# Sixteen chunks of gated linear attention in one block of 64x64 quarters, with loads issued in front of output stores

## The chip, the cores and the metric

The kernel runs on one core of a Trainium2 chip. The metric is the device time of one execution in microseconds, lower being better. Before the change the median of three runs is 465.62 us (464.9 to 467.0). Each engine of the core has its own queue of instructions: TensorE (PE, and PEld for its weight loads), VectorE (DVE), ScalarE (ACT), GpSimd (POOL) and SyncE (SP), which here only starts transfers.

## The reference

Two blocks stand one behind the other. The first is a gated linear attention with a state of 48x48 for each of 8 heads in 4 sequences of 768 positions; the second is a feed-forward block that multiplies two projections.

```
# attention, for each sequence and head
for t in range(S):
    state = alpha[t][:, None] * state + einsum(k[t], v[t])   # outer product
    y[t]  = einsum(q[t], state)
# x: (4*768, 8*48) = (3072, 384)
a = x @ w1;  b = x @ w2          # 384 -> 1024
out = (a * b @ w3) @ w_out       # 1024 -> 1024 -> 384
```

The weights of the second block come as float64 words; the kernel makes fp32 values from them and splits each into three parts, so that its large products run as exact sums of fp32r products.

## The kernel before, in words

**Chunks.** The 4 x 768 positions are cut into 24 chunks of 128 (C = 128, six chunks a sequence). The 8 heads of a chunk are 4 pairs (NP = 4): head 2j + i of pair j lies in half i of the 128 partitions, 48 of 64 used. In a chunk, cumulative sums of log alpha give a decay for every position; k divided and q multiplied by these decays make the recurrence into plain products:

- `transposed(n)`: k and q of the chunk are transposed on TensorE (L381) and copied to SBUF by ScalarE (L383, tile qkT);
- scores: k by q for each head, masked to the causal triangle by VectorE (tile ms);
- values: y = v by the masked scores, plus state by q, both summed in PSUM;
- `outer(n)`: k by v (L393), added to the state T by VectorE (L401, L403); `advance` scales the state by decays on GpSimd at every second chunk;
- ScalarE copies y out of PSUM (tile x, L489), and SyncE stores it to DRAM (tile xd, transposed as the second block wants it).

**The loop.** Lines 689 to 786 run steps n = 0 to 24. In step n the scores of chunk n are made, and the values of chunk n − 1, whose state and masked scores come from the step before. Then come the transposes of chunk n + 1, the state's update, the decays of chunk n + 3 and pieces of the second block (`run`, generators in `fill`, matmuls at L515), which fill TensorE while a chunk's small operations wait for other engines. The number of pieces goes by `n`, so some steps are long (27 matmuls of 128x384, L515) and some have none. After step 24 a second part runs only the second block.

**Chunks 8 to 23.** From TURNED = 8 on, scores use 64 x 64 pieces of TensorE, so that the quarter of the causal square that is all zero is never computed. A chunk's square is cut at position 64 into early keys and late keys: early keys meet all 128 queries, late keys only the late 64. A matmul on 64 rows and 64 columns takes one quarter of the array; the rows are the half of the partitions that its operands lie in, the columns the half of the partitions that its output goes to. Before the change step n has these groups on TensorE, in this order:

- `attend_state(n - 1)`, L474: 8 matmuls, state by q, 64 wide out, 128 columns moving, one after the other in all four quarters;
- `turned_scores(n)`, L430: for each pair, early keys (128 columns moving) and late keys (64 columns). Head i writes bank `sc[i]`, the late keys in the other half of the partitions;
- `attend_low(n - 1)`, L419, in between: early values of the early queries, 64 rows, 64 columns moving;
- `transposed(n + 1)`, L381;
- `attend(n - 1)`, L482: values of the late queries from both halves at once, 128 rows, 64 columns moving;
- `outer(n)`, L393.

For the odd heads the two halves of ms are swapped, so GpSimd makes a swapped copy of their v (`turn_v`, L167, tile vt, two buffers). Masks are four VectorE operations a chunk (L440), since the halves have different triangles. In all of this, operands in the upper half of the partitions write one PSUM bank (`y[0]`, `sc[0]`), and those in the lower half another (`y[1]`, `sc[1]`).

**Order and waits.** The source order is the order in which work is handed to a scheduler, which places instructions on each engine and sets semaphores; each engine then runs its own queue in order. PSUM has eight banks, shared by all matmuls in turn: a matmul into a bank waits until the bank's earlier content was read. `later` holds stores to be issued; `store()` empties it on SyncE. It stands at the head of the step for n = 0, 1 and from FIRST = 6 on, before the loads of alpha, k, q and v for the following chunks (`load_a`, `load_kq`, `load_v`).

Of the kernel before, what the change touches and what calls it, by code (L numbers as in the profile page):

```python
# [10 lines left out]
FP32 = mybir.dt.float32  # L11
# [37 lines left out]
def kernel(  # L49
# [30 lines left out]
    PAIRED = 8  # L80
    TURNED = 8
    assert D <= DP and DM % C == 0 and DF % CW == 0 and S % C == 0 and N % G == 0
    assert DM <= 512 and TG <= 512
# [80 lines left out]
    def turn_v(n):  # L164
        if turned(n):
            for half in range(2):
                nc.gpsimd.tensor_copy(out=vts[n % 2][ds(DP * half, DP), :, 0:D],  # L167
                                      in_=st["v", n][ds(DP * (1 - half), DP), 1::2, 0:D])

# [37 lines left out]
    keep_bc = keep[:, None, :].to_broadcast([C, NP, C])  # L207
    for half in range(2):
        nc.gpsimd.tensor_copy(out=keep_turned[ds(DP * half, DP), 1 - half], in_=keep[ds(DP * half, DP), ds(DP * half, DP)])
    nc.gpsimd.memset(keep_turned[DP:, 1], -1)  # L210
    for x in qks:
# [202 lines left out]

    def attend_low(n, jj, i, half):

        s, w = ds(DP * i, DP), (vts[n % 2] if i else st["v", n])
        h = half * NP // 2 + jj
        nc.tensor.matmul(st["y", n][0][i][ds(DP * half, DP), jj, 0:DP], w[s, h if i else 2 * h, :],  # L419
                         st["ms", n][s, i, h, 0:DP], start=(n % NCH == 0 and jj == 0), stop=True, skip_group_check=True)  # L420

    def turned_scores(n):

        qkT = st["qkT", n]
        sc = [bank().rearrange("p (j c) -> p j c", j=NP) for _ in range(2)]
        for j in range(NP):
            for part in range(2):
                for i in range(2):
                    r, t = ds(DP * i, D), slice(DP * part, C)
                    nc.tensor.matmul(sc[i][ds(DP * (part ^ i), DP), j, t], qkT[r, 0, j, ds(DP * part, DP)],  # L430
                                     qkT[r, 1, j, t], start=True, stop=True)
            if turned(n - 1):
                for i in range(2):
                    attend_low(n - 1, j % 2, i, i ^ (j < 2))
        ms = work.tile([C, 2, NP, C], FP32, tag="ms", name="ms")
        for i in range(2):
            r = ds(DP * i, DP)
            low, high = (keep_turned[r, 0], keep_turned[:, 1]) if i else (keep[r, 0:DP], keep[:, DP:])
            for x, mask, t in ((slice(DP * i, DP * (i + 1)), low, slice(0, DP)), (slice(0, C), high, slice(DP, C))):
                masked = nc.vector.tensor_tensor(ms[x, i, :, t].bitcast(I32), sc[i][x, :, t].bitcast(I32),  # L440
                                                 mask[:, None, :].to_broadcast([x.stop - x.start, NP, DP]),
                                                 op=ALU.bitwise_and)
        ends_of_part1[0] = mark["ms", n] = masked.ins
        st["ms", n] = ms

    def scores(n):
        if turned(n):
            return turned_scores(n)
        qkT = st["qkT", n]
        sc = [bank().rearrange("p (j c) -> p j c", j=NP) for _ in range(2)]  # L450
        for j in range(NP):
            for i in range(2):
                r = ds(DP * i, D)
                nc.tensor.matmul(sc[i][:, j, :], qkT[r, 0, j, :], qkT[r, 1, j, :], start=True, stop=True)  # L454
        ms = work.tile([C, 2, NP, C], FP32, tag="ms", name="ms")
        for i in range(2):
            masked = nc.vector.tensor_tensor(ms[:, i].bitcast(I32), sc[i].bitcast(I32), keep_bc, op=ALU.bitwise_and)  # L457
        ends_of_part1[0] = mark["ms", n] = masked.ins
        st["ms", n] = ms
# [17 lines left out]
    def attend(n):  # L477
        (y, heads), ms, vc = st.pop(("y", n)), st.pop(("ms", n)), st.pop(("v", n))
        for j, i, to in heads:
            if turned(n):  # L480
                w = vts[n % 2][:, j, :] if i else vc[:, 2 * j, :]
                nc.tensor.matmul(to[:, DP:], w, ms[:, i, j, DP:], start=False,  # L482
                                 stop=(j % HP == HP - 1), skip_group_check=True)
            else:
                nc.tensor.matmul(to, vc[:, 2 * j + i, :], ms[:, i, j, :], start=(n % NCH == 0 and j % HP == 0),  # L485
                                 stop=(j % HP == HP - 1), skip_group_check=True)
        x = work.tile([C, HP, 2, C], FP32, tag="x", name="x", bufs=4)
# [201 lines left out]
    for n in range(N + 1):  # L689
        if not 1 < n < FIRST:  # L690
            store()
# [13 lines left out]
        if n >= FIRST:  # L705
            load_v(n + 2)
        if n:
            attend_state(n - 1)
        if n < N:
            scores(n)  # L710
        else:
            for j in range(NP):
                for i in range(2):
                    attend_low(n - 1, j % 2, i, i ^ (j < 2))
        transposed(n + 1)
# [32 lines left out]
        turn_v(n)  # L748
        if n:
            attend(n - 1)  # L750
# [126 lines left out]
```

## Time and profile before

| what | value |
|---|---|
| median of three runs | 465.62 us |
| the profiled execution | 464.49 us |
| its span in the trace | 462.8 us |
| TensorE busy | 446.9 us, 97% |
| VectorE busy | 371.7 us, 80% |
| ScalarE busy | 276.4 us, 60% |
| GpSimd busy | 95.1 us, 21% |
| x copies L489, 128x256 | 48, 384 ns each |
| swapped copies of v L167, 64x192 | 32, 557 ns each |
| stores of x | 48 of 96 KB, 3.9 us to landing |

How to read it: the profile is one execution. A group's line names the source line, the engine, the operation, output and inputs by the program's tile names, the shape and the count, then busy time, mean duration in ns and idle time in front of it with what ended it. In a timeline a row has its start, its length, and the number of records that were merged; an fp32 matmul has two records. In a table by windows each engine has its busy time and in brackets its instructions, and then come TensorE's clock as a share of full speed, the share of the transfer engines, and GB/s. A line of waits has engine, line and who was waited for, then total us, times, and the longest. Since engines run side by side, a busy time is no share of the span by itself: what counts is which engine the others wait for.

### The profile page before, as it was taken

Reading aid. Unit: us, or ns where it says so; the run is one execution under the profiler, and the core shown is the slowest. Engines: PE = TensorE matmul, PEld = TensorE weight load, DVE = VectorE, ACT = ScalarE, POOL = GpSimd, SP = SyncE. Lnnn points to the kernel's source line nnn. Section 1 sums busy time; section 2 is a strip of 40 time slices with the busy share of each in tenths; the row PEclk is TensorE's granted clock in tenths of the full one; section 3 lists DMA queues with packets and bytes.
Section 4 is the critical chain, followed back from the end, with each engine's and each line's share of the span. In section 5 each row is a group of like instructions: output and inputs, shape, how many; then the busy total and the mean of one; then the engine's idle time right before and its main releaser. Section 6 shows DMA issues by size and latency. Waiting matters only on the chain.

```text
span 462.8 us, 11150 instructions
## 1 busy us (share of the span) xinstructions
PE 446.9 (97%) x4296; PEld 423.2 (91%) x4296; DVE 371.7 (80%) x610; ACT 276.4 (60%) x544; POOL 95.1 (21%) x186
## 2 busy tenths in 40 slices
PE   4998999999999999999999999999999999999996
PEld 2675699898999989999999999999999999999996
DVE  2779997999979988999998999997542967776671
ACT  4685975767658563988875676764545443333430
POOL 6234232325414430121221201212010000000000
PEclk9999999999999999999999999999999999999999
DMA  9999999999999974466856446412115875665511
GB/s 173 254 208 228 261 224 192 248 209 219 184 227 193 234 165 138 130 224 212 235 178 196 146 128 177 149 52 86 51 48 153 243 210 180 186 178 159 166 51 52
DMA packets 148869, 80.37 MB, mean 174 GB/s; under 512 B 97392, under 2 KB 138608, under 8 KB 148816
## 3 DMA queue, kind: packets, MB, share of 16 engines
q1 hardware_dynamic: 143040, 64.44, 57.3%
q0 software_dynamic: 5776, 15.22, 11.0%
q8 instruction: 34, 0.56, 0.5%
q14 instruction: 19, 0.16, 0.1%
HBM read 57.58 MB, written 22.06 MB: 172 GB/s over the span
## 4 chain that ended last, share of the span: by engine, by line
PE 88%; DVE 4%; DMA 4%; ACT 2%; issue 1%; SPq 0%; DVEq 0%; ACTq 0%
PE bank L515 72%; DMA kq<-in_q_dram 3%; PE bank L381 3%; PE bank L430 3%; PE bank L482 2%; PE bank L474 2%; PE bank L340 1%; PE bank L393 1%; PE bank L346 1%; PE bank L454 1%; PE bank L343 1%; PE bank L419 1%; DVE qk L359 1%; DVE ms L457 1%; PE bank L485 1%
## 5 line engine op out<-in xcount | busy, mean ns | idle before, releaser
L515 PE MATMUL bank<-x,w 128*128 128x384 f32 x1152 | 210.2, 337 | 1.7 <-ACT qkT L383 1.1
L515 PEld LDWEIGHTS bank<-x,w 128*128 128x128 f32 x1152 | 200.2, 188 | 4.1 <-ACT qkT L383 1.4
L515 PE MATMUL bank<-w3o,ab 128*128 128x384 f32 x576 | 100.2, 336 | 0.0
L515 PEld LDWEIGHTS bank<-w3o,ab 128*128 128x128 f32 x576 | 99.9, 188 | 0.0
L540 ACT ACTIVATE bank<-bank 128x384 f32<-128x384 f32 x96 | 45.6, 476 | 43.4 <-PE bank L515 43.1
L524 ACT ACTIVATE t<-bank 128x384 f32<-128x384 f32 x64 | 31.9, 499 | 54.9 <-PE bank L515 54.9
L590 POOL DMA_DIRECT2D abd<-ab x45 | 25.8, 573 | 137.9 <-DVE ab L576 121.3
L383 ACT COPY qkT<-bank 128x512 f32<-128x512 f32 x48 | 26.2, 596 | 24.8 <-PE bank L381 24.8
L641 DVE TENSOR_TENSOR ab<-abl,ab 128x1024 fp32r<-128x1024 f32 x24 | 29.3, 1223 | 12.3 <-ACT ab L640 12.3
L640 ACT ACTIVATE ab<-abl 128x1024 fp32r<-128x1024 f32 x24 | 25.5, 1061 | 20.2 <-PE bank L515 18.4
L515 PE MATMUL bank<-wo,w3T 128*128 128x384 f32 x192 | 35.9, 334 | 0.0
L576 DVE TENSOR_TENSOR ab<-bank,r 128x384 f32<-128x384 f32 x44 | 24.1, 548 | 12.5 <-PE bank L515 6.3
L515 PEld LDWEIGHTS bank<-wo,w3T 128*128 128x128 f32 x192 | 33.5, 188 | 0.0
L249 ACT ACTIVATE power<-power,rebias 128x512 uint32<-128x512 uint32 (+1 forms) x36 | 25.3, 701 | 12.6 <-DVE power L248 12.4
L359 DVE TENSOR_TENSOR qk<-kq,e 128x768 f32<-128x768 f32 x24 | 23.1, 964 | 11.3 <-ACT e L350 7.9
L526 DVE SCALAR_TENSOR_TENSOR o<-bank,t 128x384 f32<-128x384 f32 x24 | 13.4, 557 | 23.0 <-issue 13.7
L642 DVE SCALAR_TENSOR_TENSOR ab<-ab,abl 128x1024 fp32r<-128x1024 f32 x24 | 29.2, 1217 | 0.0
L526 DVE SCALAR_TENSOR_TENSOR r<-bank,t 128x384 f32<-128x384 f32 x40 | 22.0, 550 | 6.8 <-PE bank L515 3.4
L251 DVE SCALAR_TENSOR_TENSOR mant<-mant,rest 128x512 f32<-128x512 uint32 (+1 forms) x36 | 23.4, 649 | 3.7 <-ACT rest L244 3.7
L252 DVE SCALAR_TENSOR_TENSOR power<-raw,power 128x512 uint32<-128x512 uint32 (+1 forms) x36 | 23.5, 653 | 2.4 <-ACT power L249 2.4
L253 DVE TENSOR_TENSOR mant<-mant,power 128x512 f32<-128x512 f32 (+1 forms) x36 | 23.6, 655 | 0.5
L244 ACT ACTIVATE rest<-raw 128x512 f32<-128x512 uint32 (+1 forms) x36 | 23.3, 649 | 0.0
(102 smaller groups left out, 675.2 us busy)
## 6 DMA issues: line engine op xcount, KB each, us to landing
abl<-abd SPq DMA_DIRECT2D x24, 512.0 KB, 4.7
abd<-ab POOLq DMA_DIRECT2D x45, 192.0 KB, 3.2
raw<-in_moe_w_dram SPq DMA_DIRECT2D x64, 128.0 KB, 3.4
raw<-in_moe_w_dram SPq DMA_DIRECT2D x12, 512.0 KB, 5.8
xT<-xd POOLq DMA_DIRECT2D x9, 576.0 KB, 4.7
kq<-in_k_dram SPq DMA_DIRECT2D x24, 192.0 KB, 5.2
kq<-in_q_dram SPq DMA_DIRECT2D x24, 192.0 KB, 5.4
xd<-x SPq DMA_DIRECT2D x48, 96.0 KB, 3.9
```

The costliest lines, as they stand in the source:

```text
L249: nc.scalar.activation(power, power, AF.Relu, scale=2.0 ** 23, bias=rebias)
L359: mark["qk", n] = nc.vector.tensor_mul(qks[n % 3][:, :, :, 0:D], st.pop(("kq", n)), st.pop(("e", n)).rearrange("p i (h d) -> p i h d", h=H ...
L383: mark["qkT", n] = nc.scalar.copy(qkT[:, :, :, ds(DP * half, DP)], tp[half]).ins
L515: nc.tensor.matmul(p, w[part][i], x[part][i], start=start and part == parts[0] and i == 0, stop=stop and part == parts[-1] and i == n - 1, ...
L524: nc.scalar.activation(t, p1, AF.Copy, scale=(1.0 + 1.0 / P) * scale)
L526: nc.vector.scalar_tensor_tensor(to, p2, scale, t, op0=ALU.mult, op1=ALU.add)
L540: nc.scalar.activation(p, p, AF.Copy, scale=1.0 + 1.0 / P)
L576: nc.vector.tensor_mul(ab, p, r[0])
L590: (nc.gpsimd if late else nc.sync).dma_start(out=abd[g][:, f, :], in_=ab)
L640: nc.scalar.activation(t[:, 0], ab, AF.Copy, scale=1.0 - 2.0 ** -13)
L641: nc.vector.tensor_sub(t[:, 1], ab, t[:, 0].bitcast(FP32))
L642: nc.vector.scalar_tensor_tensor(t[:, 2], t[:, 0].bitcast(FP32), -1.0 - 1.0 / P, ab, op0=ALU.mult, op1=ALU.add)
```

## The change

For the steps n = 9 to 24 all attention matmuls of a step come as one block, `attention(n)`, made of two lists that are merged by their cost:

- `quarters(n - 1)` gives state, early values and late values of chunk n − 1, each as pairs of 64x64 matmuls, one for either head of a pair. Pairs 0 to 2 (LQ = 3) take the quarters that cross: rows of half i, columns of half 1 − i, and bank `y[0]`. Pair 3 takes the straight quarters, rows and columns of half i, and bank `y[1]`.
- `quarter_scores(n)` gives the scores of chunk n, all in the straight quarters: early keys into bank `sc[0]`, late keys into `sc[1]`.

Step 8 has the new scores alone, and step 24 the new values alone; `scores`, `attend_state` and `attend` stay for the chunks before 8.

With the scores of head i always in half i, GpSimd's copy of v now holds the early half of odd heads and the late half of even heads; it is still two copies a chunk. The masks are two operations instead of four: one over 128x512 and one over 128x256. The copies of y to x are 128x384 and 128x128 instead of twice 128x256, placed where `attend` stood. Both halves of the partitions now write the same bank, each in its own half of the bank's partitions. A chunk's x goes to DRAM in four stores instead of two. And for n above 8, `store()` is called after the step's loads.

```diff
@@ quarters and attention, in place of attend_low and turned_scores
+    def quarters(n):
+        ms, vc, vt, qkT = st.pop(("ms", n)), st.pop(("v", n)), vts[n % 2], st.pop(("qkT", n))
+        y = [bank()[:, 0:x * C].rearrange("p (j c) -> p j c", c=C) for x in (LQ, NP - LQ)]
+        first, state = set(), n % NCH > 0
+        def add(j, i, w, x, t):
+            at = j >= LQ
+            to = y[at][ds(DP * (i if at else 1 - i), DP), j - LQ * at, t]
+            nc.tensor.matmul(to, w, x, start=(at, i) not in first, stop=True, skip_group_check=True)
+            first.add((at, i))
+        def steps(heads):
+            for j in heads * state:
+                yield 2, [(j, i, Ts[n % 2][ds(DP * i, D), j, :], qkT[ds(DP * i, D), 1, j, :], slice(0, C)) for i in range(2)]
+            for j in heads:
+                yield 2, [(j, i, vt[DP:, j, :] if i else vc[0:DP, 2 * j, :], ms[ds(DP * i, DP), 0:2, j, :], slice(0, C))
+                          for i in range(2)]
+            for j in heads:
+                yield 1, [(j, i, vc[DP:, 2 * j + 1, :] if i else vt[0:DP, j, :], ms[ds(DP * i, DP), 2, j, :], slice(DP, C))
+                          for i in range(2)]
...
+        def copied():
+            x = work.tile([C, NP // 2, 2, C], FP32, tag="x", name="x", bufs=4).rearrange("p j i c -> p (j i) c")
+            for a, b in zip(y, (x[:, 0:LQ], x[:, LQ:])):
+                mark["x"] = ends_of_part1[1] = nc.scalar.copy(b, a).ins
...
+                later.append((to[1 - half, :, 0:LQ], x[s, 0:LQ]))
+                later.append((to[half, :, LQ:], x[s, LQ:]))
...
+    def quarter_scores(n):
         qkT = st["qkT", n]
+        sc = [bank().rearrange("p (e j c) -> p e j c", e=2, j=NP), bank()[:, 0:NP * DP].rearrange("p (j c) -> p j c", j=NP)]
+        def score(x):
+            j, late = x
+            for i in range(2):
+                r, to = ds(DP * i, D), ds(DP * i, DP)
+                q = qkT[r, 1, j, ds(DP * late, DP)] if late else qkT[r, 1, j, :].rearrange("p (e c) -> p e c", e=2)
+                nc.tensor.matmul(sc[1][to, j, :] if late else sc[0][to, :, j, :], qkT[r, 0, j, ds(DP * late, DP)], q,
+                                 start=True, stop=True)
...
+    def attention(n):
+        low, high = quarters(n - 1) if turned(n - 1) else ([], [])
+        done = None
+        if n < N:
+            own, done = quarter_scores(n)
+            high = own + high
+        low, high, at = deque(low), deque(high), [0, 0]
+        while low or high:
+            k = 0 if not high or low and at[0] <= at[1] else 1
+            cost, f, x = (low, high)[k].popleft()
+            at[k] += cost
+            f(x)
+        if done:
+            done()
@@ the loop
-        if not 1 < n < FIRST:
+        if not 1 < n < FIRST and n <= TURNED:
             store()
...
         if n >= FIRST:
             load_v(n + 2)
-        if n:
+        if n > TURNED:
+            store()
+        if 0 < n <= TURNED:
             attend_state(n - 1)
-        if n < N:
+        if n < TURNED:
             scores(n)
         else:
-            for j in range(NP):
-                for i in range(2):
-                    attend_low(n - 1, j % 2, i, i ^ (j < 2))
+            attention(n)
         transposed(n + 1)
...
         turn_v(n)
-        if n:
+        if n > TURNED:
+            st.pop(("x", n - 1))()
+        elif n:
             attend(n - 1)
```

## The prediction, made before the changed kernel ran

> **What bounds the kernel now.** I read the page first: busy times, clock, the chain that ended last.
>
> ```profile
> PE 446.9 (97%) x4296; PEld 423.2 (91%) x4296; DVE 371.7 (80%) x610; ACT 276.4 (60%) x544; POOL 95.1 (21%) x186
> PEclk9999999999999999999999999999999999999999
> PE 88%; DVE 4%; DMA 4%; ACT 2%; issue 1%; SPq 0%; DVEq 0%; ACTq 0%
> ```
>
> TensorE is busy for 97% of the span at its full clock, and the chain runs through it. The change lies in the steps n = 8 to 24, about 68 to 185 us. For that stretch I took the busy times from 60 to 185 us and TensorE's own waits from 60 to 182 us.
>
> ```profile
> 60.00:185.00 125.00, 122.78 (x2121) 113.25 (x2120) 113.10 (x218) 79.53 (x181) 40.00 (x75) 1.00 0.94 204
> ```
> ```profile
> PE bank L515 <- ACT qkT L383: 1.1, 1, 1.1
> PE bank L515 <- DVE ms L440: 0.5, 1, 0.5
> PE bank L474 <- DVE ms L440: 0.3, 1, 0.3
> PE bank L430 <- ACT w L260: 0.2, 1, 0.2
> ```
>
> TensorE works 122.8 of 125 us there and waits 2.1 us in four places. VectorE, at 113.1 us, is next, and two of the four are waits for its masks. So a microsecond of TensorE work moves the end, and work taken off other engines is worth those 2.1 us at most. The timeline of TensorE then shows one step with a state (n = 9), the step after a new sequence (n = 13) and the last one:
>
> ```profile
> 76.59 0.67 PE L474 MATMUL bank<-qkT,T 48*64 48x128 f32 x16
> 77.08 0.38 PE L430 MATMUL bank<-qkT 48*64 48x128 f32 x7
> ...
> 78.15 0.22 PE L419 MATMUL bank<-ms,vt 64*64 64x64 f32 x1
> 78.29 0.71 PE L381 MATMUL bank<-ident,qk 64*128 64x64 f32 x16
> 78.93 0.34 PE L482 MATMUL bank<-ms,v 128*64 128x64 f32 x4
> ...
> 79.45 0.62 PE L393 MATMUL bank<-v,qk 128*64 128x48 f32 x16
> 80.00 0.62 PE L346 MATMUL bank<-la,sums 128*128 128x384 f32 x2
> ...
> 106.20 0.44 PE L430 MATMUL bank<-qkT 48*64 48x128 f32 x8
> 107.46 0.71 PE L381 MATMUL bank<-ident,qk 64*128 64x64 f32 x16
> ...
> 183.07 0.67 PE L474 MATMUL bank<-qkT,T 48*64 48x128 f32 x16
> 184.57 15.72 PE L515 MATMUL bank<-x,w 128*128 128x384 f32 x89
> ```
>
> Every fp32 matmul has two records, its two passes. What the reader is to see is that four quarters of the array run side by side: 8 state matmuls, two for each quarter, take 0.49 us. So the time of a block is that of its fullest quarter.
>
> **The prices.** The two passes of a 64-wide matmul start 0.06 us apart (L419: 77.20 and 77.26), so it costs 0.12. Before, the fullest quarter of scores and early values holds four 128-wide and two 64-wide matmuls. Its last pass ends at 78.15 + 0.06 = 78.21, so 1.13 − 0.24 = 0.89 us is for four wide ones: 0.22 each. The state's 0.49 is two wide ones, 0.44, and 0.05 for starting in a new tiling. From the last pass to the transposes is 0.08.
>
> **TensorE's work, step by step.** Removed in a step with a state: state 0.49, scores with early values 1.21, and the late values behind the transposes 0.52; 2.22 us. Added: one block. The quarters that cross (rows of one half, columns of the other) hold state, early and late values of three heads' pairs, 3 × (0.22 + 0.22 + 0.12) = 1.68. The straight ones hold four scores and the fourth pair, 4 × 0.34 + 0.56 = 1.92. The block is 0.05 + 1.92 + 0.08 = 2.05. The outer product now comes first in its tiling and pays the 0.04 that the late values paid (0.52 less eight passes of 0.06). So 2.09 against 2.22: −0.13, in 13 steps, −1.7 us.
> - n = 13 and 19 have no state. Before 1.26 + 0.52 = 1.78 (the late values taken as at n = 9); after, the straight quarter 1.36 + 0.34 = 1.70, with 0.17 of ends 1.87: +0.1 each.
> - n = 8 has scores alone. They took 0.98 (68.24 to 69.22 in the timeline), all four quarters in use; now they are in two, 1.36 + 0.08: +0.46.
> - n = 24 has values alone: 1.50 before, after 0.05 + 1.68 + 0.08 + 0.04 = 1.85: +0.35.
>
> Sum: −1.7 + 0.2 + 0.46 + 0.35 = −0.7 us. The number of matmuls and the columns that they stream are the same; only the packing gains, and the two ends give half of it back.
>
> **VectorE.** Four masks become two per chunk:
>
> ```profile
> L457 DVE TENSOR_TENSOR ms<-bank,keep 128x512 int32<-128x512 int32 x16 | 10.3, 682 | 0.7 <-PE bank L454 0.5
> ```
> ```profile
> L440 DVE TENSOR_TENSOR ms<-bank,keep_turned 64x256 int32<-64x256 int32 x16 | 6.8, 428 | 0.5
> ```
>
> The four L440 forms have means of 428, 425, 408 and 406 ns, 1.67 us. The new pair is 682 (L457) and about 415: 1.10. Over 16 chunks that is −9 us of VectorE, hidden behind TensorE except at the waits above. Of those 2.1 us the change can leave all or none. The scores' banks are read out 0.5 us sooner and the y banks are copied before the transposes are done, where they were held past the late values. I take two thirds: −1.4.
>
> **ScalarE.** 256 + 256 columns become 384 + 128, the same sum: nothing, with TensorE 97% busy as cover; without cover 0.1 us a step. But the copies of x now stand in front of those of qkT (in the order of the built program). In short steps (10, 14, 18, 22) TensorE has 0.55 + 0.04 + 0.55 = 1.14 us of work between the transposes and the next block, whose second instruction now needs the new qkT; before, it came 0.49 later. The x copies (0.63 to 0.66 us for two) end about when the transposes do, then the qkT pair takes 1.07. That gives waits of about 0.1 in four steps, +0.4; bounds 0 and 4 × 0.55 = 2.2, if another ScalarE row of that size stands in between.
>
> **GpSimd.** Two copies of 64x192 before and after: nothing. Its outputs are needed as early as before.
>
> **SyncE and the transfers.** A chunk's x goes out in four stores, not two, 32 triggers more. The page's packets stay. A pair of stores takes 0.86 to 0.95 us of the queue, so +0.9 a step, with 28 us of listed waits in that queue between 60 and 182 us to take it up. The loads of a step pass its stores, and what was behind the wait for the copies of x (6.2 us in all) no longer is. The tightest load is v of chunk 14: landed at 111.9 (GpSimd's copy waits for it), used by the outer product at 113.41, 1.5 us to spare. Two earlier steps' extra triggers delay it by 1.8, its own stores, now behind it, give back 0.9: 0.6 is left. I take nothing, with 1 us above as bound. The xT loads keep their places ahead of the step's stores, and the stores that they read are a step old.
>
> **Unseen.** Two things have no row. (1) The two row halves of the array now write one PSUM bank, in different partitions; before, each half had its own bank. The nearest row is the outer product L393, where two column halves share a bank and a pass starts every 0.07 us: no cost. If pairs could not overlap at all, a block would take 2 × 1.92: +1.9 us in 15 steps, +1.4 at n = 8, +1.7 at n = 24: +32. I take 0, the nearer row, since partitions differ there too. (2) Early scores write, and early values read, two runs of 64. For reading, L340 has runs of 48 and the same shortest record (486 ns) as the contiguous L343: nothing. For writing, at most 0.02 per matmul, as two 64-wide ones: 0 to +1.3 us, taken as 0.
>
> [...]
>
> **Sum.** −0.7 − 1.4 + 0.4 = −1.7 us. The profiled execution took 464.49 us (span 462.8 and 1.7 around it), 1.1 below the median of 465.62; 462.8 for it, 463.9 as a median.
>
> **The rivals.**
> - Waits fall away wholly. VectorE is 90% busy in the stretch, and small delays of L515 that no wait line shows (18 of them took 3.62 us at 113.96 and 3.39 at 122.83) are some 0.6 us more. −0.7 − 2.1 − 0.6 = −3.4: 462.2. Against it: the 1.1 us wait is for ScalarE's qkT copy, behind a weight conversion that stays.
> - Slower by a new wait: the second instruction of each block waits for qkT or a score bank, and TensorE's order holds the rest behind it. The place is L466's first row. With the upper bounds, 2.2 there and 1 for v, and a third of the old waits gone, −0.7 − 0.7 + 3.2 = +1.8; with 1.3 for the writes +3.1: 467.4 to 468.7. It decides where the waits in front of the block pass 1.4 us in all. Against it: qkT was ready 0.9 us early at n = 10.
> - Slower by the shared bank: 465.6 + 30 = 496. It decides as soon as a twentieth of the overlap is lost (1.7 of 32).
> - The change does nothing: the packing gain is eaten by the ends (−0.7 alone): 464.9.
>
> **How the numbers follow.** Of a change below 0.5% (2.3 us) a measurement of this kernel can hardly tell. Chances: the forecast with the last rival 0.47, of which 0.10 lies below 463.3 by its own spread; waits gone 0.26, nearly all faster; new wait 0.19, of which 0.04 stays within the bound; shared bank 0.08. So faster 0.35, same 0.42, slower 0.23. The range leaves out the shared bank, the last twentieth of the new waits and a twentieth below: 461.3 to 468.7.
>
> **What would show it.** Right: the block from its first state matmul to the transposes takes 2.0 to 2.1 us, the transposes are followed at once by L395, the masks are two rows of about 680 and 415 ns, and TensorE's waits between 60 and 185 us fall below 1.5 us. Wrong: a block of 2.3 us or more (a quarter waits: look at the gaps between L466's passes), rows of 128 columns starting over 0.11 us apart in one quarter (the bank), or L466 with waits for ScalarE's qkT.

## The result and the profile after

The changed kernel takes 469.75 us (median of 6 runs, 468.19 to 471.63), the kernel before 464.72 us. The ratio is 1.0105, with a 95% interval of 1.0073 to 1.0138: slower by 1%, where 463.9 us had been forecast and 468.7 was the upper end of the range. The profiled execution of the changed kernel took 470.62 us (span 468.9), against 464.49 for the one of before.

First the page of the changed kernel: busy times, granted clock, the chain that ended last.

```profile
PE 449.2 (96%) x4296; PEld 426.0 (91%) x4296; DVE 362.4 (77%) x578; ACT 277.7 (59%) x544; POOL 92.4 (20%) x186
PEclk9999999999998999999999999999999999999999
PE 82%; DVE 4%; DMA 4%; SPq 4%; ACT 3%; issue 2%; DVEq 0%; ACTq 0%
```

VectorE has lost the 9 us that were worked out (371.7 to 362.4). But TensorE's share of the chain fell from 88% to 82%, and SyncE's queue, which had none, now has 4%. One slice of the clock row is an 8.

Then the stretch of the change, by the busy times from 60 to 185 us (columns: PE, PEld, DVE, ACT and POOL busy, granted clock, share of the transfer engines, GB/s), and TensorE's waits from 60 to 195 us:

```profile
60.00:185.00 125.00, 118.74 (x2050) 110.24 (x2050) 99.69 (x176) 78.92 (x176) 37.57 (x75) 0.99 0.92 190
```
```profile
PE bank L348 <- DVE la L331: 2.7, 1, 2.7
PE bank L395 <- DMA v<-in_v_dram: 2.0, 1, 2.0
PE bank L556 <- DVE ms L473: 0.7, 1, 0.7
PE bank L466 <- ACT t L565: 0.6, 1, 0.6
PE bank L466 <- DVE ms L473: 0.2, 1, 0.2
```

The four waits of before are gone from their places. Instead there stand a wait for the logarithms of alpha (`la`), one for v, and smaller ones: 6.2 us where there were 2.1. The list holds only idle times of TensorE above 0.15 us; a wait that hides behind running matmuls is not in it, and one such comes up further down. In a step that follows a long one, the block is what the forecast made it. TensorE's timeline in the step n = 9:

```profile
77.16 0.33 PE L426 MATMUL bank<-qkT,T 48*64 48x128 f32 x2
77.17 0.33 PE L466 MATMUL bank<-qkT 48*64 48x128 f32 x2
...
79.21 0.71 PE L383 MATMUL bank<-ident,qk 64*128 64x64 f32 x16
79.86 0.67 PE L395 MATMUL bank<-v,qk 128*64 128x48 f32 x16
```

From the first state matmul to the transposes 79.21 − 77.16 = 2.05 us, as forecast; L395 follows at once. VectorE's masks are two groups of 16, 128x512 at 681 ns and 128x256 at 412 ns in the mean.

**Where the time went.** I laid the two traces side by side at the start of each chunk's transposes. The table gives how much later than in the kernel before they start (us; minus is earlier). The transposes of chunk k stand in step k − 1. The last two columns belong to experiments further down (`x_both` and `r_twohead`). In the changed kernel and in the block alone, the values of the late queries (0.52 us) now stand in front of the transposes and not behind them, so from chunk 10 on about +0.5 of each of their rows is this, save the last row.

| transposes of chunk | before, at | changed | queue edits alone | block alone |
|---|---|---|---|---|
| 8 | 57.09 | +0.11 | −0.73 | −0.12 |
| 10 | 78.29 | +0.92 | −0.72 | +0.68 |
| 12 | 92.31 | −0.63 | −0.68 | −0.16 |
| 15 | 112.25 | −0.45 | +0.13 | −0.34 |
| 16 | 121.12 | +2.61 | +1.38 | −0.15 |
| 18 | 136.91 | +2.34 | +2.48 | −0.42 |
| 19 | 140.60 | +7.29 | +3.15 | +0.00 |
| 23 | 168.35 | +7.32 | +5.27 | +0.36 |
| last matmul | 459.10 | +6.12 | +4.76 | −0.84 |

In the changed kernel the time is lost in two places, between the transposes of chunks 15 and 16 (+3.06) and of 18 and 19 (+4.95). Elsewhere it gains or holds, once the +0.5 of place and the +0.46 that was forecast for n = 8 are taken off the row of chunk 10.

**What stands behind the two places.** SyncE's queue, by its timeline in the kernel before (a step's loads and stores, from one load of alpha to the next):

```profile
104.72 0.41 SPq L147 DMA_DIRECT2D ac<-in_alpha_dram  x1
105.18 0.67 SPq L153 DMA_DIRECT2D kq<-in_k_dram  x1
105.91 1.32 SPq L154 DMA_DIRECT2D kq<-in_q_dram  x1
107.34 0.64 SPq L159 DMA_DIRECT2D v<-in_v_dram  x1
108.02 1.68 SPq L236 DMA_DIRECT2D raw<-in_moe_w_dram  x1
109.80 0.38 SPq L590 DMA_DIRECT2D abd<-ab  x1
110.27 0.95 SPq L305 DMA_DIRECT2D xd<-x  x2
111.33 0.46 SPq L147 DMA_DIRECT2D ac<-in_alpha_dram  x1
```

The same step in the changed kernel:

```profile
106.55 0.41 SPq L148 DMA_DIRECT2D ac<-in_alpha_dram  x1
107.01 0.69 SPq L154 DMA_DIRECT2D kq<-in_k_dram  x1
107.76 1.95 SPq L155 DMA_DIRECT2D kq<-in_q_dram  x1
109.82 1.21 SPq L160 DMA_DIRECT2D v<-in_v_dram  x1
111.08 3.52 SPq L307 DMA_DIRECT2D xd<-x  x4
114.64 0.43 SPq L238 DMA_DIRECT2D raw<-in_moe_w_dram  x1
115.17 0.38 SPq L631 DMA_DIRECT2D abd<-ab  x1
115.66 0.38 SPq L148 DMA_DIRECT2D ac<-in_alpha_dram  x1
```

The reader is to see two things. In both kernels one trigger (the instruction that starts a transfer) begins where the last ends: the queue has no empty time (in the kernel before, from 70 to 170 us, only three gaps pass 0.2 us, 2.5 us in all), and triggers of 1 to 3 us stand beside others of 0.4 us for the same kind of load. And the stores grew from 0.95 to 3.52 us, so the next load of alpha goes out 9.1 us after the last, not 6.6. It adds up: the alpha load of chunk 21 is issued at 132.91 before and at 139.35 after, 6.4 us later, at a time when TensorE itself is 2.3 us later. The v of chunk 14 was issued at 107.34 and is now at 109.82; it lands at 114.42 instead of 111.78, and L395 waits for it.

The second place, by the chain that ended last in the changed kernel:

```profile
131.11 2.75 SPq L155
133.97 0.79 SPq L160
134.81 2.07 SPq L307
...
137.88 0.43 SPq L307
138.41 3.41 DMA abd<-ab
141.91 0.12 DVE ab L604
```

Four stores stand in front of a store of `abd`. That one frees a buffer that VectorE's L604 writes. VectorE's timeline shows what is behind it:

```profile
141.91 0.56 DVE L604 TENSOR_TENSOR ab<-r 128x384 f32<-128x384 f32 x1 [4.31 <-DMA abd<-ab]
142.38 0.55 DVE L331 TENSOR_TENSOR la<-la,la 128x384 fp32r<-128x384 f32 x1
```

VectorE stood for 4.31 us, and L331, the second half of `la`, could not pass it; ScalarE's half (L330) had begun at 137.36. So the wait for `la` is not for alpha but for a store two queues away. TensorE's 2.65 us of idle time cost more than themselves, as the granted clock then shows (same columns as above):

```profile
144.00:145.00 1.00, 0.88 (x14) 0.52 (x10) 1.00 (x3) 1.00 (x4) 0.00 (x0) 0.50 1.36 197
...
147.00:148.00 1.00, 1.00 (x32) 0.93 (x26) 1.00 (x3) 0.25 (x1) 0.00 (x0) 0.79 0.34 67
```

From 144.0 to 147.4 us TensorE ran at half its clock. The block of that step (n = 18) took 4.53 us, 143.36 to 147.89, where the kernel with light loads further down (`ll_after`) takes 2.72: its second instruction came 1.10 us after the first, behind masks that VectorE, late as well, began at 143.72, and most of the rest ran at half clock.

### The profile page after: what moved, and what is told of

The parts are those of the page before. It is cut to its first block, busy times and chain, and to the rows that moved or that the text cites. A ratio compares the mean times of both kernels' runs of the same rounds, so it can differ in the third digit from the quotient of the medians.

```text
span 468.9 us, 11152 instructions
## 1 busy us (share of the span) xinstructions
PE 449.2 (96%) x4296; PEld 426.0 (91%) x4296; DVE 362.4 (77%) x578; ACT 277.7 (59%) x544; POOL 92.4 (20%) x186
## 4 chain that ended last, share of the span: by engine, by line
PE 82%; DVE 4%; DMA 4%; SPq 4%; ACT 3%; issue 2%; DVEq 0%; ACTq 0%
PE bank L556 68%; PE bank L426 3%; PE bank L383 2%; PE bank L466 2%; DMA ac<-in_alpha_dram 2%; DMA kq<-in_q_dram 2%; PE bank L395 2%; SPq L307 1%; PE bank L500 1%; DVE qk L361 1%; PE bank L345 1%; PE bank L342 1%; SPq L155 1%; DVE r L567 1%; DMA abd<-ab 1%
## 5 line engine op out<-in xcount | busy, mean ns | idle before, releaser
L565 ACT ACTIVATE t<-bank 128x384 f32<-128x384 f32 x64 | 31.4, 494 | 55.4 <-PE bank L556 55.4
L466 PE MATMUL bank<-qkT 48*64 48x128 f32 (+1 forms) x512 | 26.6, 255 | 0.9 <-ACT t L565 0.6
L426 PE MATMUL bank<-ms,v 64*64 64x64 f32 (+1 forms) x256 | 25.8, 251 | 0.1
L466 PEld LDWEIGHTS bank<-qkT 48*64 48x64 f32 x512 | 23.9, 139 | 1.6 <-ACT t L565 0.8
```

The lines of the kernel that those rows point to most:

```text
L426: nc.tensor.matmul(to, w, x, start=(at, i) not in first, stop=True, skip_group_check=True)
L466: nc.tensor.matmul(sc[1][to, j, :] if late else sc[0][to, :, j, :], qkT[r, 0, j, ds(DP * late, DP)], q, start=True, stop=True)
L565: nc.scalar.activation(t, p1, AF.Copy, scale=(1.0 + 1.0 / P) * scale)
```

## The experiments

My theory after the traces: the block is a gain, and the loss is made by SyncE's queue, which was full before; doubled stores and the new order make loads, and stores that others wait for, late. Rivals: the order alone; the doubled stores alone; new waits in front of the block on TensorE's, ScalarE's and VectorE's own order, whatever the queue does.

**1. The parts alone.** The doubled stores in the kernel before:

```diff
-            later.append((to[half, :, :, ds(c * C, C)], x[ds(DP * half, D)]))
+            for h in (slice(0, 3), slice(3, NP)) if turned(n) else (slice(0, NP),):
+                later.append((to[half, :, h, ds(c * C, C)], x[ds(DP * half, D), h]))
```

> The kernel before with nothing changed but the stores of x of chunks 8 to 23: each of a chunk's two stores is cut into two (three heads and one head), so 32 triggers more on SyncE, the same bytes, the old array layout and the old order. Theory (triggers): SyncE's queue falls behind by about 0.43 us for each trigger, the loads of alpha and v issue several us late from step 12 on, TensorE waits for them: 468 to 472 us, against 464.7 before. Rival (order of loads and stores): this kernel keeps the old order, so 464 to 466. Rival (new waits in front of the block on TensorE's own order, for the copies of qkT, x and the masks): no block here, 464 to 466.

The order in the kernel before:

```diff
-        if not 1 < n < FIRST:
+        if not 1 < n < FIRST and n <= TURNED:
             store()
...
             load_v(n + 2)
+        if n > TURNED:
+            store()
```

> The kernel before with nothing changed but the place of the stores: in steps after n = 8 SyncE issues the step's loads first and then the stores of the chunk before. Two stores a chunk, old array layout. Theory (triggers): no trigger is added, so 463.5 to 465.5 us. Rival (order): the order alone brings the loss, 467 to 471. Rival (waits in front of the block): 464 to 466.

The changed kernel with the order put back (this diff the other way round):

> The changed kernel with the stores put back to the head of the step, in front of the loads; four stores a chunk and the block of quarters stay. Theory (triggers): the queue is as full as in the changed kernel, 468 to 473 us. Rival (order): the loss goes, 461.5 to 464.5. Rival (waits in front of the block): 468 to 471, with waits on qkT, x copies and masks and none on loads.

The changed kernel with two stores a chunk:

```diff
-            for a, b in zip(y, (x[:, 0:LQ], x[:, LQ:])):
-                mark["x"] = ends_of_part1[1] = nc.scalar.copy(b, a).ins
+            nc.scalar.copy(x[:, 0:LQ], y[0])
+            for i in range(2):
+                mark["x"] = ends_of_part1[1] = nc.scalar.copy(x[ds(DP * i, D), LQ:], y[1][ds(DP * (1 - i), D)]).ins
...
-                later.append((to[1 - half, :, 0:LQ], x[s, 0:LQ]))
-                later.append((to[half, :, LQ:], x[s, LQ:]))
+                later.append((to[1 - half], x[s]))
```

> The changed kernel with two stores a chunk instead of four: ScalarE copies the fourth pair's values out of its bank in two copies of 64 partitions (48 used) that swap the halves, so that each half of the partitions holds eight rows sets that one store takes. One ScalarE instruction more a step (an estimate from the 128-column copy of the changed kernel: 0.2 to 0.3 us). Block of quarters and loads before stores stay. Theory (triggers): SyncE keeps up again, 461.5 to 464.5 us. Rival (order): 468 to 471. Rival (waits in front of the block): 468 to 472, since ScalarE has more to do ahead of the copies of qkT.

Measured, as ratios to the kernel before (464.8 us beside them): doubled stores 467.68 us, 1.0065 (1.0039 to 1.0090); order 465.98, 1.0025 (1.0008 to 1.0043); changed kernel with the old order 467.26, 1.0068 (1.0044 to 1.0092); with two stores 468.40, 1.0084 (1.0058 to 1.0109). Each edit of the queue costs something without the block, the doubled stores 2.9 us. But neither theory in its simple form holds: taking back one edit alone gives back 2.5 us (the order) or 1.4 us (the stores) of 5.0. My forecast of 461.5 to 464.5 for two stores was a miss, and its 468.40 lies in the ranges of both rivals; the doubled stores and the old order came out just under the 468 that the theory had as lower end, and the order alone above its 465.5.

**2. Other queues.** If SyncE's issuing is short, another engine could issue the stores. In the changed kernel, with a queue beside each entry of `later`:

```diff
-            dst, src = later.popleft()
-            nc.sync.dma_start(out=dst, in_=src)
+            dst, src, queue = later.popleft()
+            queue.dma_start(out=dst, in_=src)
```

> The changed kernel with its four stores a chunk (chunks 8 to 23) issued by GpSimd in place of SyncE, at the same point of the step. The bytes and the packets stay; SyncE has 64 triggers less than in the changed kernel and 32 less than before. Theory A (SyncE's issuing is what falls behind: each trigger holds it for 0.38 to 0.45 us at the least): the loads go out earlier than before, 461.5 to 465. Theory B (the transfers themselves are the bound in steps 8 to 18: the transfer engines are busy for 0.94 of 60 to 185 us before, so what the new block gains turns into waits for loads): 464 to 467, no better than the kernel before. Rival (new waits in front of the block): 468 to 471 as the changed kernel.

> The changed kernel with its four stores a chunk (chunks 8 to 23) issued by ScalarE in place of SyncE, at the same point of the step; ScalarE made the copies that they read a step before, so it waits for nothing. Theory A (SyncE's issuing falls behind): 461.5 to 465, unless the triggers hold ScalarE (4 a step) ahead of the copies of qkT, then 465 to 468 with waits of TensorE for ScalarE. Theory B (the transfers are the bound): 464 to 467.

GpSimd: 469.85 us, 1.0103 (1.0068 to 1.0137). ScalarE: 475.73 us, 1.0248 (1.0225 to 1.0272). Both were misses for the theory. GpSimd's time lies in the range of the rival of new waits (468 to 471), and its longest wait is in front of a block, but the moved triggers make it. GpSimd's timeline, and TensorE's longest wait there:

```profile
163.53 2.21 POOL L307 DMA_DIRECT2D xd<-x  x4
165.79 0.73 POOL L168 COPY vt<-v 64x192 f32<-64x192 f32 x2
166.60 0.50 POOL L414 TENSOR_TENSOR T<-tmp,dec 128x192 f32<-128x192 f32 x1
```
```profile
PE bank L426 <- POOL T L414: 3.7, 1, 3.7
```

The four triggers, 2.21 us, and the copies of v stand in front of the state (L414) that the next block begins with. On ScalarE they stand in front of the copies of qkT, and TensorE's longest wait there is for these:

```profile
PE bank L466 <- ACT qkT L385: 5.0, 3, 4.3
```

So the four stores cannot simply be put elsewhere: each of these queues has something behind them that TensorE needs soon.

**3. Fewer packets.** Are the long triggers a queue that the transfers hold up? The loads of k and q move runs of 192 bytes. Here they are read as runs of 1536, with as many triggers and bytes. The values then come in another order, so these kernels are probes and none to keep:

```diff
-        nc.sync.dma_start(out=st["kq", n][:, 0], in_=rows(k, n))
-        nc.sync.dma_start(out=st["kq", n][:, 1], in_=rows(q, n))
+        for i, src in enumerate((k, q)):
+            flat = src[b].rearrange("h s d -> (h s d)")[ds(c * C * DM, C * DM)].rearrange("(p x) -> p x", p=C)
+            nc.sync.dma_start(out=st["kq", n][:, i].rearrange("p h d -> p (h d)"), in_=flat)
```

first from chunk 12 on:

> The kernel before with k and q of chunks 12 to 23 loaded as 128 contiguous runs of 1536 bytes instead of 1024 runs of 192 bytes: as many triggers and as many bytes, about a third of the packets of a step gone. These chunks get k and q values in another order (they compute on other numbers; all instructions stay). Theory A (triggers): transfers were hidden before, 464 to 465.5. Theory B (transfers are the bound of the stretch, beside TensorE): the kernel before gains a little, 462 to 464.5, since it is held by TensorE as well.

> The changed kernel with the same edit of the loads of k and q of chunks 12 to 23 (1536-byte runs, values in another order, all instructions and triggers stay). Theory A (SyncE's triggers: 0.38 to 0.45 us each whatever they move): the loss stays in the main, 467 to 470. Theory B (transfers are the bound, and long triggers are a queue that is held up by full transfer engines): the loss goes and the gain of the block shows, 460.5 to 463.5, that is 1.5 to 3 below the kernel before with the same edit. Rival (new waits in front of the block): 468 to 471.

The kernel before did not move: 464.66 us, 1.0001 (0.9985 to 1.0016). The changed one came down from 469.75 to 465.04, 1.0002 (0.9978 to 1.0025): the loss is gone with the triggers all there. That contradicts a fixed price for each trigger. SyncE's timeline of this kernel:

```profile
101.48 0.42 SPq L161 DMA_DIRECT2D kq<-in_k_dram  x1
101.95 0.44 SPq L161 DMA_DIRECT2D kq<-in_q_dram  x1
102.50 0.38 SPq L166 DMA_DIRECT2D v<-in_v_dram  x1
102.93 3.44 SPq L313 DMA_DIRECT2D xd<-x  x4
```

The loads' triggers are 0.38 to 0.44 us in these lines. The four stores still take 3.44, and the queue still has little empty time (4.8 us in gaps from 70 to 170), but it runs less late: v of chunk 14, the third line, is issued at 102.50, where it was 109.82. But the block's gain, 1.5 to 3 us by the theory, was not in the medians. Part of it is in the profiled executions: from the transposes of chunk 8 to the last matmul the changed kernel takes 400.2 us and the one before 401.9. What the changed one lost lies ahead of the change, where its granted clock was 0.50 from 50.9 to 57.8 us. Then I took the loads of k and q from chunk 2 on, and those of alpha from chunk 8 on, the same way:

> The kernel before with all k and q loads from chunk 2 on, and the alpha loads from chunk 8 on, as 128 runs of 1536 bytes in place of 1024 of 192: nearly all short packets but those of v are gone, triggers and bytes stay, the values come in another order. It serves as the ground for the next kernel: TensorE's order without the pressure of the loads. Both theories: 459 to 464.5, with less spread from run to run than before, as the waits in the first 60 us shrink too.

> The changed kernel with the same edit of the loads. Theory B (the block of quarters gains what was worked out, and the loss of the changed kernel is all from late loads): 1.5 to 3 us below the kernel before with the same edit. Rival (the block's gain is eaten by new waits on ScalarE's and VectorE's order, whatever the loads do): within 0.7 us of it, or slower.

Before 464.57 us, 1.0000 (0.9982 to 1.0018); changed 461.75, 0.9936 (0.9919 to 0.9954), 2.8 us less. (The runs of the first still spread over 3.5 us, where a smaller spread had been expected: five at a mean clock of 1.00 took 462.7 to 464.2, seven at 0.992 to 0.995 took 464.3 to 466.2.) In the profiled executions some of the difference lies ahead of the change: from the transposes of chunk 8 to the last matmul the second gains 2.4 us on the first. This is the block's gain, with its order on all engines, where the queue has room (26 us of gaps from 70 to 170). New waits there are, but the rival that they make the loss falls. TensorE's waits in the second, from 60 to 195 us, are one line:

```profile
PE bank L567 <- DVE ms L484: 0.8, 1, 0.8
```

**4. The block alone.** The changed kernel with two stores, at the head of the step (the last two of the first group at once), and the same with v loaded ahead of k and q:

> The changed kernel with two stores a chunk (ScalarE swaps the halves of the fourth pair in two copies) and the stores back at the head of the step: only the block of quarters is left of the change, and one ScalarE copy more a step. Theory B (late loads): 463 to 466, since the queue is as in the kernel before and the block makes the steps shorter, so that some loads come late again. Rival (the order is of no account, the block itself loses): 467 to 470, like the changed kernel with two stores.

```diff
+        if n > TURNED:
+            load_v(n + 2)
         for m in (n + 3,) * (n <= FIRST) + (n + 4,) * (n >= FIRST):
...
-        if n >= FIRST:
+        if FIRST <= n <= TURNED:
             load_v(n + 2)
```

> As the kernel with two stores at the head of the step, and v of chunk n + 2 is loaded ahead of k and q of chunk n + 4 in steps after 8, so that the load that is needed first goes first. Theory B (late loads): 461.5 to 464.5, no waits of TensorE for v. If k, q or alpha come late in its place: 464 to 467. Rival (the block itself loses): 467 to 470.

The block alone: 462.98 us, 0.9967 (0.9945 to 0.9989), faster than both kernels. With v first: 464.33, 0.9989 (0.9974 to 1.0005), no better, so v's place in the step is not the point.

**5. The queue alone, and the prices beside the block.** Still open was whether the two queue edits make the whole loss without the block, and what each costs beside it, since the kernels had run in different sets and their runs spread over 3 us. `x_both` is the kernel before with the first two diffs of the first group; the others were run again beside it.

> The kernel before, old array layout, with both edits of SyncE's queue and nothing else: four stores a chunk (chunks 8 to 23) and, after n = 8, the step's loads ahead of the stores. Theory B (the loss of the changed kernel is made by the queue alone): as slow as the changed kernel or slower, 468 to 471, since the single edits cost about 3.0 and 1.2 and the block is not there to gain 1.5. Rival (the loss needs the block, whose steps are shorter): no more than the sum of the two, 467 to 469, and below the changed kernel.

> A second set of runs of the kernel with the block, two stores a chunk, and loads ahead of stores, beside the next two on the same chip. Theory (the place of the stores costs several us once the block makes the steps shorter): 467 to 469, 4 to 6 above the same with the stores at the head. Rival (the first set had bad luck in its first 60 us, where the change does nothing): 464 to 466.

> A second set of runs of the kernel with the block, four stores a chunk at the head of the step. Theory (the doubled triggers cost some 4 us beside two stores at the head): 466.5 to 468. Rival (luck): 464 to 466.

> A second set of runs of the kernel with the block alone: two stores a chunk at the head of the step. Theory: 462.5 to 464, 1 to 2 below the kernel before. Rival (luck in the first set): 464 to 466.

| | stores | place | us | ratio to before (95%) |
|---|---|---|---|---|
| old layout (first set) | 4 | head | 467.68 | 1.0065 (1.0039 to 1.0090) |
| old layout (first set) | 2 | behind loads | 465.98 | 1.0025 (1.0008 to 1.0043) |
| old layout | 4 | behind loads | 469.27 | 1.0101 (1.0081 to 1.0120) |
| block | 2 | head | 463.72 | 0.9984 (0.9967 to 1.0000) |
| block | 4 | head | 468.69 | 1.0088 (1.0067 to 1.0108) |
| block | 2 | behind loads | 467.75 | 1.0064 (1.0044 to 1.0083) |
| block (the change) | 4 | behind loads | 469.75 | 1.0105 (1.0073 to 1.0138) |

The queue's edits alone are as slow as the whole change: 1.0101 and 1.0105. Without the block they cost 2.9 and 1.2 us, and 4.9 together; within the intervals they add. Beside the block, either of them alone costs 4.0 to 5.0 us (r_two and r_head against r_twohead; 5.4 and 4.3 in the first sets, so which costs more is open), and both about 6, with the change itself taken from another set. The chains of the two, by engine, first the queue alone and then the block alone:

```profile
PE 75%; DVE 7%; DMA 6%; SPq 6%; ACT 3%; issue 2%; POOL 1%; DVEq 0%; ACTq 0%; POOLq 0%
```
```profile
PE 88%; DMA 6%; DVE 4%; ACT 1%; SPq 1%; issue 1%; DVEq 0%; ACTq 0%
```

With the queue edits alone, SyncE's queue holds 6% of the chain; with the block alone 1%, and TensorE's waits from 60 to 195 us in it are two:

```profile
PE bank L556 <- DVE ms L473: 0.8, 1, 0.8
PE bank L395 <- DMA v<-in_v_dram: 0.2, 1, 0.2
```

The expected ranges held for three of these four; four stores at the head came out above theirs (466.5 to 468).

Why either queue edit costs more beside the block than without it was not settled. The granted clock has a part in it: its mean over the runs is 0.996 and 0.997 in r_head and r_two, against 0.999 in r_twohead. The block alone is not free of ScalarE either: it has one copy more in each step than the change (the fourth pair in two copies of 261 ns, where one took 275), and its blocks in the short steps 10, 18 and 22 take 2.51, 2.92 and 2.86 us, against 2.12, 2.72 and 2.67 in `ll_after`.

## Why the prediction was wrong, step by step

**The step that failed is "SyncE and the transfers", which was taken as nothing, with 1 us above as bound.** The runs price it at 4.9 us without the block (x_both) and about 6 beside it (469.75 against 463.72). Three things in it were wrong.
- "28 us of listed waits in that queue ... to take it up" were not empty time. In SyncE's timeline of the kernel before, triggers stand end to end, and many of 1 to 3 us are held up. With a third of the packets gone the triggers of the loads shrink, of q from 1.7 to 0.5 us in the mean and of v from 0.9 to 0.4 (l_after against the kernel before, 70 to 170 us). The row that I quoted for the stretch had said as much, a share of 0.94 for the transfer engines, and I read only TensorE's column of it.
- The delay was counted over two steps and for one load. It is carried from step to step, as the queue has no room to catch up: 6.4 us on the alpha load of chunk 21.
- "A pair of stores takes 0.86 to 0.95 us of the queue, so +0.9 a step" was the price of five pairs at the head of a step, from 81 to 111 us. Other pairs of the same trace took 2.21, 1.28, 2.01 and 1.90 us (at 69.82, 116.61, 122.36 and 130.92). Four stores behind the loads, where the queue is fullest, took 3.5 us: +2.6.

"The tightest load is v of chunk 14" named the first stall rightly: L395 waited 1.96 us there, where 0.6 was to be left to spare. The larger stall, behind a store of `abd` and VectorE's L604, was not in the sum: I costed the loads behind the stores, and not the other stores in that queue. And nothing stood in it for the clock.

**TensorE's work, −0.7: right.** The block takes 2.05 us with a state (2.05 forecast) and 1.83 without one at n = 13 (105.54 to 107.37; 1.83); n = 24 takes 1.81 (1.85). The exceptions belong to ScalarE, below.

**VectorE, −9 us: right** (−9.3), with masks of 681 and 412 ns.

**The old waits, −1.4 of 2.1: right in size.** They are gone, and 0.8 to 1.0 us of others is left where the queue is not in the way (ll_after, r_twohead). Work and waits together had been put at −2.1, or −1.7 with the copies of x. The block alone measured −1.5 and −0.7, and −2.8 where the loads are light (−2.4 in the profiled pair, without what lies ahead of chunk 8). That these lie on both sides of −1.7 is in part luck, since the next term was too small; how the measured gains split was not worked out.

**ScalarE, +0.4: right in kind, too small by 1 us.** No wait of a block for qkT is listed in the changed kernel, since matmuls of the state run on meanwhile, but it is in the timelines. ScalarE and TensorE of the changed kernel at n = 22:

```profile
172.50 1.07 ACT L385 COPY qkT<-bank 128x512 f32<-128x512 f32 x2 [0.23 <-PE bank L383]
```
```profile
172.99 0.87 PE L426 MATMUL bank<-qkT,T 48*64 48x128 f32 x12
173.62 0.55 PE L466 MATMUL bank<-qkT 48*64 48x128 f32 x8
```

The block's first instruction starts at 172.99 and its second, which needs the new qkT, at 173.62, when the copies have ended (173.57); at n = 9 the two were 0.01 apart. The block takes 2.67 us. "In short steps (10, 14, 18, 22) TensorE has 0.55 + 0.04 + 0.55 = 1.14 us of work between the transposes and the next block" holds for 10 and 14 alone. In front of n = 22 no sums of logarithms (L348) are left to make, and in front of n = 18 the outer product is missing, as chunk 18 begins a new sequence. In `ll_after` the four blocks take 2.12, 2.12, 2.72 and 2.67 us where others take 2.06, together +1.4, inside the bound of 2.2.

L466's listed 0.6 us in the changed kernel is for `t` of L565, which stood behind the logarithm of an alpha that landed at 120.33, late by the queue.

**The shared bank, 0: right, and it was the largest risk.** Quarters of both row halves write one bank, in different partitions, in the block of 2.05 us. If pairs had not overlapped, it would be 1.9 longer. They ran side by side: at 77.87 us two passes of L426, one from either row half, start together and write the one bank `y[0]`, and the next two follow 0.11 us later. **The strided write, 0: right**: L466's 128-wide passes start 0.11 us apart, as the contiguous state's do.

The rival "slower by a new wait" had the sign and, at 467.4 to 468.7, nearly the size, but it put the place at the block's second instruction and the cause in qkT and the score banks. Waits for qkT are there and cost about 1.4 us, but they are in the fast versions too; the loss is at L395 and L348, and its cause is SyncE's queue.

## What to carry to other kernels

The queue of transfers had no room where its triggers stood end to end (2.5 us of gaps from 70 to 170 us), whatever its list of waits said (28 us): look at the timeline of the issuing engine and the share of the transfer engines before you add a trigger or move one behind large loads. In the full queue here a delay was kept from step to step (6.4 us on the alpha load of chunk 21), so count it to the last step and follow everything that is queued behind it, the stores that free buffers too. A list of idle times does not show an instruction that waits while earlier matmuls still run (at n = 22 the block's second began 0.63 us after its first, which the list does not have): compare the length of the same block in all steps. When one change joins a gain and a cost, take the gain alone: the block with two stores at the head of the step is the fastest version here that reads its values in their order (0.9967 and 0.9984 of the kernel before, in two sets of runs), though only by 0.7 to 1.5 us.

## What the runs showed of the hardware

**Stalls of like length halved the clock in one place and not in another.** After the idle 2.65 us at 140 to 143 us the granted clock fell to 0.50 from 144.00 to 147.41. In the second set of runs with four stores at the head, TensorE was idle from before 144 to after 146, waiting for v, and the clock was 0.75, 0.50 and 0.90 in the three stretches of 2 us from 146 on. Idle times of 1.96 us (the changed kernel at 112.5) and 2.8 us (four stores at the head, first set, at 113.7) left it at 1.00.

The clock records of the traces tell some of these apart. In the changed kernel the clock is 1.00 from its first record at 17.71 to 144.00, 0.50 to 147.41, and 1.00 again to 468.27, behind the last matmul: 126.29, 3.41 and 320.85 us, which are 37, 1 and 94 times 3.413. In the kernel before it is 1.00 from 17.09 to 464.24: 447.15 us, 131 times 3.413. Six other stretches at half clock, read from tables by 2 us, are about 3.4 us long (from 89.5 us in `e_scalar` and 147.0 in `r_head`) or 6.8 (from 116.8 in `e_scalar` again, 166.0 in `e_gpsimd`, 37.5 in `e_two`, 50.9 in `l_after`). So in the two traces the clock changes at borders that lie whole multiples of 3.413 us apart. Cut into pieces of that length, by PE's busy time, the stall of 2.65 us has 2.40 in the piece from 140.59 to 144.00, and half clock follows. The 1.96 us fall on two pieces, with 0.88 and 1.19 us idle (109.87 to 113.28 to 116.69), and full clock follows; so it does in the kernel before after 1.03 us (85.36 to 88.77) and 1.73 (457.41 to 460.83). The amount alone does not decide it: in `l_after` half clock begins at 50.9, though TensorE was idle for only 1.5 us in all from 46 to 52. How the 2.8 us fell on such pieces is not shown. The pieces begin at other times in the two traces (17.09 and 17.71 us), so the same stall may fall on them in another way in another execution; that was not tested. A piece at half clock is 3.41/2 = 1.7 us of TensorE's work, an estimate from its length.

The mean granted clock of the six runs of the changed kernel was 0.993 (0.988 to 0.996); of the kernel before it was 0.9975 to 0.999 in the four sets of 17 to 25 runs. TensorE bounds the kernel (busy for 96 and 97% of the two spans), so 0.45 to 0.6% of clock is 2.1 to 2.8 us of the 5.0, an estimate from these means. It is not needed for the loss: the kernel with the queue edits alone lost 4.9 us at 0.998.

**Packets, not triggers or bytes, filled the queue.** With the bytes and the triggers kept and the runs of k and q at 1536 bytes instead of 192, the share of the transfer engines from 60 to 185 us fell from 0.94 to 0.82 in the kernel before (204 and 205 GB/s), and the whole loss of the changed kernel went (469.75 to 465.04 us). Per 100 us (60 to 160) the packets fell from 67,646 to 47,145.
